# Last sums by column halves, and slots in two parts around a w_in product

## The chip, the core and the metric

The kernel runs on one core of a Trainium2 chip. The core has a matrix engine (TensorE, PE in the profile; PEld is its weight load), VectorE (DVE), ScalarE (ACT), GpSimd (POOL), SyncE (SP, which here only issues DMAs) and 16 DMA engines. SBUF is the on-chip memory with 128 partitions, PSUM holds matmul results in banks. The metric is the device time of one execution in microseconds. Before the change it is 702.29 us, the median of three runs (701.78 to 702.86).

## The reference

For 8 images with 8 heads each, 576 tokens and head size 64, `phi` (576 x 32 per head) is turned into weights by a softmax over the tokens. The weights gather keys and values into 32 memory slots per head; queries attend to the slots; the result, as rows of 512 numbers, goes through an ELU network.

```python
a = exp(phi - max(phi, axis=2)); a = a / (sum(a, axis=2) + 1e-9)
k_m = einsum('bhsm,bhsd->bhmd', a, k)          # 32 slots per head
v_m = einsum('bhsm,bhsd->bhmd', a, v)
attn = softmax(scale * q @ k_m.T)              # over the 32 slots
x = (attn @ v_m) as (4608, 512)
h = x @ w_in                                   # (512, 2048)
g = where(h > 0, h, exp(min(h, 0)) - 1)
out = g @ w_out                                # (2048, 512)
```

## The kernel before

Attention output and `w_in` are never multiplied as such. Per image the kernel forms `vw`, the product of the value slots with `w_in` (L798), in four quarters of 512 columns, and then the hidden rows as probabilities times `vw` (`hidden`, L845). Values that need more than one pass are split into a high and a low part, and products are three passes (HI·HI, LO·HI, HI·LO, the list PASSES).

**Iterations.** From image 2 on each image takes 32 iterations: two halves of 288 tokens, 16 blocks of 128 hidden channels each. `hidden` makes 12 matmuls of 288 columns into one of two banks named psh; ScalarE and VectorE form the ELU (L869, L870, L881, L889); L901 and L907 make the high and low part `gp` of the first 256 tokens; `project` (L923) multiplies both 128-token tiles with `w_out` in 12 matmuls of 512 columns (L915), summed over the 16 blocks in four banks named pso. The last 32 tokens of each half go into a `rest` tile by L889. Over two images there are four such strips of 32, together 128 rows.

**The rest.** After every second image `rest_high` and `rest_low` split two channel blocks at a time, and `rest_project` (L968) adds six matmuls of 512 columns into bank pso00 for each of eight such pairs, 48 in all. `rest_store` (L976) copies the bank into a tile `orest` (L978, ScalarE) and stores it with four DMAs of 32 rows (L982), all four on SP, or, for the last two images, two on SP and two on ACT. Ahead of that the last tiles of the last image are copied (L945, L947) and stored by L950.

**Joint stretches.** Products with 64 rows and 32 columns of weights stand in groups between two projections. In the second such group of images 3 to 6 (`o = base + 2.9`, L1110 on) stand 16 matmuls for quarter 2 of `vw` into the pso banks "y" and "z", 16 for quarter 3 into the two psh banks ("hh"), 144 for the slots of the next image (`next_slots`, L636, into two psb banks, through `slots`, L491 and L505), and 16 for the last scores of this image (`scores_last`, L646), which use the free part of the same psb banks. The copies of the two quarters follow on ScalarE (L810) and VectorE (L816).

**Order.** All orders are written out: the list FIRST up to image 2, and behind it steps with a place, `at(place, step, ...)`, sorted by place and, at one place, by the order of the calls. Each engine runs its instructions in that order; waits between engines come from the tiles that the instructions use.

Of the kernel before, what the change touches and what calls it, by code (L numbers as in the profile page):

```python
# [12 lines left out]
ALU = mybir.AluOpType  # L13
# [3 lines left out]
P = 128  # L17
B, H, S, D, M = 8, 8, 576, 64, 32
DM, DFF = 512, 2048
HALF = S // 2  # L20
NT = HALF // P
REST = HALF - NT * P
# [6 lines left out]
NCH = 5  # L29
NPAIR = H // 2  # L30
NBL = S // 64
NJ = DFF // P
# [142 lines left out]
def fused_kernel(ctx: ExitStack, tc: tile.TileContext, phiT, phi, kv0, kvt, kv, kvb, q0, q1, w_in, w_out, out):  # L175
# [8 lines left out]
    nc = tc.nc  # L184
# [13 lines left out]
    wout = {}  # L198
    def t2k(shape, name):
        return work.tile(shape, F32, name=name, tag="t2k", bufs=7)  # L200
# [47 lines left out]
    def bank(shape, where):  # L248

        pool, name = {  # L250
            "b": (ps_b, "psb"), "h": (ps_h, "psh"),
            "w": (ps_o, "pso00"), "x": (ps_o, "pso01"),
            "y": (ps_o, "pso10"), "z": (ps_o, "pso11"),
        }[where]
        return pool.tile(shape, F32, name=name)
# [17 lines left out]
    def of_blocks(t, u):  # L273
        return t.rearrange("p c (d x) -> p (c d) x", d=2)[:, : min(4, NBL - 4 * u)]
# [48 lines left out]
    def rows_in(b, c, a):  # L323
        r = rows_of(c)
        return slice(a * r, a * r + r) if r < P else slice(0, r)

    def kv_rows(b, c, i, head):
        rows = rows_in(b, c, head % 2)
        if c == 4:
            t = st[b]["kv"]["T" if b == 0 else 4][rows, 0]  # L330
            return t.rearrange("p (i j) d -> p i j d", i=2)[:, i[0] : i[-1] + 1, head // 2, :]
        if b:
            return st[b]["kv"][c][rows, i[0] : i[-1] + 1, head, :]
        return st[0]["kv"]["KV"[i[0]] + str(c // 2)][rows, c % 2 : c % 2 + 1, head, :]
# [156 lines left out]
    def slots(b, c, i=(0, 1), where="bb"):  # L491

        s = st[b]
        if c == 0 and ("slots", i) not in s["ps"]:
            s["ps"]["slots", i] = [bank([P, len(i), D], x) for x in where]
        ps = s["ps"]["slots", i]
        if b >= NB:
            t = s["kv"][c].rearrange("p i h d -> p (i h d)")
            t = t.rearrange("p (c i j d) -> p c i j d", c=2, i=2, j=NPAIR)
            for k in range(2 * c, min(2 * c + 2, NBL)):  # L500
                e = of_blocks(s["e"][k // 4], k // 4)[:, k % 4]
                for a in range(2):
                    for j in range(NPAIR):
                        r = slice(64 * a, 64 * a + 64)
                        nc.tensor.matmul(  # L505
                            ps[a][32 * j : 32 * j + 32],
                            e[r, 32 * j : 32 * j + 32],
                            t[r, k % 2, :, j],
                            start=(k == 0),
                            stop=(k == NBL - 1),  # L510
                            tile_position=(64 * a, 32 * j),
                            skip_group_check=True,
                        )
            return
        for a in range(2):
            rows = rows_in(b, c, a)
            for j in range(NPAIR):
                x = a * P + j * M
                nc.tensor.matmul(
                    ps[a][32 * j : 32 * j + 32],  # L520
                    s["e"][c // 2][rows, c % 2, x : x + M],
                    kv_rows(b, c, i, 2 * j + a),
                    start=(c == 0),
                    stop=(c == NCH - 1),
                    tile_position=(rows.start, 32 * j),
                    skip_group_check=True,
                )
# [108 lines left out]
    def next_slots(b):  # L636

        both = [bank([P, UT + 2 * D], "b") for _ in range(2)]
        st[b]["both"] = both
        st[b + 1]["ps"]["slots", (0, 1)] = [  # L640
            x[:, UT:].rearrange("p (i d) -> p i d", i=2) for x in both
        ]
        for c in range(NCH):
            slots(b + 1, c)

    def scores_last(b):  # L646
        both = st[b].pop("both", None) or [bank([P, UT], "h") for _ in range(2)]
# [186 lines left out]
    gs = {}  # L834
# [75 lines left out]
    acc = {}  # L910
    osbs = {}

    def by_channels(ps, gp, j, first, last):
        for n, (x, y) in enumerate(PASSES):
            nc.tensor.matmul(  # L915
                ps,
                gp[:, y],
                wout[j][:, x, :],
                start=(first and n == 0),
                stop=(last and n == 2),  # L920
            )
# [40 lines left out]
    def rest_low(p, i):  # L962
# [2 lines left out]
            gp[:, LO], gf.rearrange("p j n -> p (j n)"), gp[:, HI], ALU.subtract  # L965
        )

    def rest_project(p, i):  # L968
        if i == 0:
            acc["rest", p] = ps_o.tile([P, DM], F32, name="pso00")  # L970
        gp = gs.pop(("rest", p, i))[1]
        for n in range(2):
            j = 2 * i + n
            by_channels(acc["rest", p], gp[:, :, n * P : (n + 1) * P], j, j == 0, j == NJ - 1)

    def rest_store(p):  # L976
        t = t2k([P, DM], "orest")
        nc.scalar.copy(t, acc.pop(("rest", p)))  # L978

        eng = (nc.sync, nc.scalar) if p == B // 2 - 1 else (nc.sync, nc.sync)  # L980
        for n in range(4):
            eng[n % 2].dma_start(  # L982
                out[2 * p + n // 2, n % 2, NT * P :], t[n * REST : (n + 1) * REST, :]
            )

    tiny = work.tile([P, 1], F32, name="tiny", bufs=1)
    work.tile([P, 24], F32, name="pad_tiny", bufs=1)
# [42 lines left out]
    first = []  # L1030
# [9 lines left out]
    def at(place, f, *a):  # L1040
        if (f, a) not in done:
            plan.append((place, len(plan), f, a))
# [14 lines left out]
    def copies(b, c, *places):  # L1057
        for a, x in enumerate(places):
            at(x, vw_high, b, c, 0, CW, (a,))
            at(x, vw_low, b, c, 0, CW, (a,))  # L1060
# [17 lines left out]
    def slots_done(b, o, *steps):  # L1078
        copied, turned, q_at = (o + x for x in steps)
        at(copied, slots_copy, b)  # L1080
        at(turned, slots_transpose, b)
        at(turned + 0.1, kv_copy, b)
        for u in range(NU):
            at(q_at + u, load_q, b, u)
# [11 lines left out]
    for b in range(3, B):  # L1096
        base = 2 * NJ * b
        o = base - 10.1
        at(o, vw, b, 1, 0, CW, "bb")
        at(o, vw, b, 0, 0, CW, "hh")  # L1100
        at(o, scores_first, b, "wx")
        for c in (1, 0):
            copies(b, c, o, o)
        softmax(b, 0, base - 9.2, 0, 1, 2, 3, 4, 5)
        softmax(b, 1, base - 7.7, 0, 1, 2, 3, 4, 5)
        if b + 1 < B:
            summaries(b + 1, base, -21, -18, -17, -8.2, -16.2, -14, -13)
            slots_done(b + 1, base, 4.3, 7.4, 6)
        softmax(b, 2, base + 1.7, None, 0, 1, 2, 3, 4)
        o = base + 2.9  # L1110
        at(o, vw, b, 2, 0, CW, "yz")
        if b + 1 < B:
            at(o, vw, b, 3, 0, CW, "hh")
            at(o, next_slots, b)
            at(o, scores_last, b)
        else:
            at(o, scores_last, b)
            at(o, vw, b, 3, 0, CW, "bb")
        copies(b, 2, o, o)
        if b + 1 == B:  # L1120
            at(o, turn, b, 3)
        copies(b, 3, o, o)
        softmax(b, 3, base + 5.3, 0 if b + 1 < B else None, 1, 2, 3, 4, 5)
        behind |= {base - 8, base - 7}
        if b + 1 < B:
            behind |= {base + 6, base + 7}
    for it, (b, hf, j) in enumerate(order):
        o = it - 1.35 if it in behind else it - 1.7
        if b > NB:
            o -= 0.96 * (it % 2)  # L1130
        at(o, hidden, it)
        at(o + 0.01, elu_exp, it)
        at(o + 0.02, elu_max, it)
        if b < NB:
            at(it - 1.67, rest_copy, it)
        elif b > NB and b % 2 == 0 and order[max(it - 2, 0)][0] != b:
            at(32 * b - 0.34 + 0.005 * (it - 32 * b), elu_rest, it)
        else:
            at(o + 0.03, elu_rest, it)
        late = 0.695 if it and b != order[it - 1][0] and b % 2 == 0 and b > NB else 0  # L1140
        at(it - 1 + late, elu_high, it)
        at(it - 0.99 + late, elu_low, it)
        at(it + 0.6, project, it)
        if ends[it][2]:
            for t in range(NT):
                at(it + 0.7, collect, it, t)
            if j == NJ - 1:
                at(it + 0.8, store, b, hf)
                if b % 2 and hf:
                    for i in range(NJ // 2):  # L1150
                        at(it + 0.61 + 0.01 * i, rest_high, b // 2, i)
                        at(it + 0.611 + 0.01 * i, rest_low, b // 2, i)
                        at(it + 0.612 + 0.01 * i, rest_project, b // 2, i)
                    at(it + 0.81, rest_store, b // 2)

    plan.sort(key=lambda x: x[:2])
# [50 lines left out]
```

## Time and profile before

| | |
|---|---|
| median of three runs | 702.29 us |
| the profiled execution | 702.28 us |
| its span, first to last instruction | 700.3 us |
| PE, PEld busy | 690.1, 579.7 us |
| DVE, ACT, POOL busy | 460.1, 445.5, 66.2 us |
| HBM read, written | 53.77, 9.44 MB |

The times in the profile are counted from the start of the span. A matmul's busy time includes its way through the array, so several overlap; how fast they follow one another is read from the length of a run of them. A name such as `psb<-kvt,e` gives the tile written and the tiles read.

### The profile page before, as it was taken

To read this page: it belongs to the slowest core of one execution; us is meant where nothing else is said; L and a number is where in the kernel's file an instruction comes from. 1 tells how busy PE (TensorE), PEld (TensorE's weight loads), DVE (VectorE), ACT (ScalarE), POOL (GpSimd) and SP (SyncE) were. 2 spreads that over 40 slices of the span, in tenths; PEclk is the share of its full clock that TensorE was granted. 3 is DMA by queue.
4 is the path that set the end of the run, shared out by engine and by line. 5 is a ranking of instruction groups with operands and counts; after the bars stand their busy time and mean duration, and the time that the engine had idled before them with its cause. 6 is when DMAs were issued, how large, how long until landed. Compare 5 with 4: busy or idle time off the path is not lost.

```text
span 700.3 us, 14400 instructions
## 1 busy us (share of the span) xinstructions
PE 690.1 (99%) x5496; PEld 579.7 (83%) x5496; DVE 460.1 (66%) x1264; ACT 445.5 (64%) x1106; POOL 66.2 (9%) x111
## 2 busy tenths in 40 slices
PE   8999999999999999999999999999999999999997
PEld 7778887888868888888887887888888888878886
DVE  4989887977696558576664666766674655766442
ACT  3879988877457576656655566655664555666552
POOL 0332352123001010001000010000100000000000
PEclk9999999999999999999999999999999999999999
DMA  9992014341404451123202232030501200000001
GB/s 337 407 364 91 1 42 143 101 146 42 137 31 134 168 181 47 49 85 120 85 1 60 90 112 92 31 103 3 174 29 46 69 1 31 1 31 1 30 1 46
DMA packets 24220, 64.14 MB, mean 92 GB/s; under 512 B 3288, under 2 KB 4824, under 8 KB 24152
## 3 DMA queue, kind: packets, MB, share of 16 engines
q1 hardware_dynamic: 23480, 63.06, 25.8%
q8 instruction: 44, 0.72, 0.4%
q10 hardware_dynamic: 672, 0.16, 0.1%
q14 instruction: 24, 0.20, 0.1%
HBM read 53.77 MB, written 9.44 MB: 90 GB/s over the span
## 4 chain that ended last, share of the span: by engine, by line
PE 94%; DMA 4%; DVE 0%; issue 0%; ACT 0%; SPq 0%
PE pso L915 57%; PE psh L854 29%; PE psb L578 3%; PE psb L505 2%; DMA raw<-w_out 2%; PE pso L578 2%; DMA raw<-w_in 1%; PE psh L578 1%; DMA qh<-q 1%; DMA touch<-kv 0%; PE psb L591 0%; PE pso L591 0%; PE psb L547 0%; PE psh L734 0%; SPq L321 0%
## 5 line engine op out<-in xcount | busy, mean ns | idle before, releaser
L915 PE MATMUL pso<-wout,gp 128*128 128x512 f32 x1728 | 426.8, 393 | 0.0
L915 PEld LDWEIGHTS pso<-wout,gp 128*128 128x128 f32 x1728 | 314.2, 188 | 66.5 <-issue 4.0
L854 PEld LDWEIGHTS psh<-A,vw 128*128 128x128 f32 x1536 | 218.4, 188 | 19.4 <-DVE gp L907 2.5
L854 PE MATMUL psh<-A,vw 128*128 128x288 f32 x1536 | 230.4, 295 | 0.7 <-ACT A L777 0.4
L869 ACT ACTIVATE gf<-psh 128x288 f32<-128x288 f32 x256 | 104.6, 409 | 120.8 <-PE psh L854 118.0
L881 DVE SCALAR_TENSOR_TENSOR gf<-gf,psh 128x256 f32<-128x256 f32 x192 | 80.3, 418 | 115.9 <-ACT gf L870 115.8
L907 DVE TENSOR_TENSOR gp<-gf,gp 128x256 fp32r<-128x256 f32 x256 | 113.2, 445 | 29.0 <-ACT gp L901 27.0
L901 ACT CAST gp<-gf 128x256 fp32r<-128x256 f32 x256 | 101.5, 401 | 34.1 <-DVE gf L881 17.3
L870 ACT ACTIVATE gf<-gf 128x288 f32<-128x288 f32 x256 | 113.9, 445 | 8.1
L293 POOL TENSOR_TENSOR e<-e,nmb 128x512 f32<-128x512 f32 (+1 forms) x18 | 19.1, 1081 | 291.9 <-DMA e<-phi 97.6
L878 DVE SCALAR_TENSOR_TENSOR gf<-gf,psh 128x288 f32<-128x288 f32 x64 | 28.5, 450 | 17.1 <-ACT gf L870 15.4
L889 DVE SCALAR_TENSOR_TENSOR rest<-gf,psh 128x32 f32<-128x32 f32 x192 | 34.6, 180 | 0.0
L816 DVE TENSOR_TENSOR vw<-psb,vw 128x512 fp32r<-128x512 f32 (+2 forms) x40 | 20.9, 561 | 14.3 <-ACT vw L810 14.3
L959 ACT CAST gp<-rest 128x256 fp32r<-128x256 f32 x32 | 13.0, 406 | 25.1 <-PE pso L915 25.1
L964 DVE TENSOR_TENSOR gp<-rest,gp 128x256 fp32r<-128x256 f32 x32 | 13.3, 421 | 18.8 <-ACT gp L959 18.5
L897 POOL COPY rest<-gf 128x32 f32<-128x32 f32 x64 | 18.7, 319 | 71.2 <-DVE gf L878 71.2
L810 ACT CAST vw<-psb 128x512 fp32r<-128x512 f32 (+2 forms) x40 | 17.5, 488 | 11.8 <-PE psb L578 11.6
L395 ACT ACTIVATE mag<-raw 128x512 uint32<-128x512 uint32 x30 | 20.0, 669 | 2.7 <-DVE win L417 1.4
L391 ACT ACTIVATE mag<-raw 128x512 f32<-128x512 f32 x30 | 19.7, 667 | 1.3 <-DMA raw<-w_in 1.0
L578 PE MATMUL psb<-win,kvm 64*32 64x512 f32 (+2 forms) x320 | 17.9, 505 | 0.0
L816 DVE TENSOR_TENSOR vw<-pso,vw 128x512 fp32r<-128x512 f32 (+1 forms) x18 | 10.1, 597 | 9.9 <-ACT vw L810 9.8
L505 PEld LDWEIGHTS psb<-kvt,e 64*32 64x32 f32 x864 | 12.6, 105 | 3.3 <-issue 3.3
(144 smaller groups left out, 474.1 us busy)
## 6 DMA issues: line engine op xcount, KB each, us to landing
kvt<-kvb SPq DMA_DIRECT2D x24, 512.0 KB, 4.8
raw<-w_in SPq DMA_DIRECT2D x15, 512.0 KB, 8.0
raw<-w_out SPq DMA_DIRECT2D x15, 512.0 KB, 10.0
out<-osb SPq DMA_DIRECT2D x14, 512.0 KB, 2.8
qt<-q SPq DMA_DIRECT2D x18, 384.0 KB, 4.3
kvt<-kv SPq DMA_DIRECT2D x8, 512.0 KB, 8.9
ph<-phiT SPq DMA_DIRECT2D x7, 576.0 KB, 5.6
e<-phi SPq DMA_DIRECT2D x12, 256.0 KB, 3.4
```

The lines of the kernel that those rows point to most:

```text
L505: nc.tensor.matmul(ps[a][32 * j : 32 * j + 32], e[r, 32 * j : 32 * j + 32], t[r, k % 2, :, j], start=(k == 0), stop=(k == NBL - 1), tile_p ...
L578: nc.tensor.matmul(outs[a][32 * j : 32 * j + 32, :], lhs[r, 32 * j : 32 * j + 32], rhs[r, j], start=True, stop=True, tile_position=(64 * a ...
L816: nc.vector.tensor_tensor(t[:, LO, a, n0:n1], s["ps"]["vw", c, n0][a], t[:, HI, a, n0:n1], ALU.subtract)
L854: nc.tensor.matmul(ps, t[:, x, g, c0 : c0 + P], s["A"][hf][:, y, g, :], start=(n == 0), stop=(n == 5),)
L869: nc.scalar.activation(gf, ps, AF.Relu, scale=-1.0)
L870: nc.scalar.activation(gf, gf, AF.Exp, scale=-1.0)
L878: nc.vector.scalar_tensor_tensor(gf, gf, -1.0, ps, ALU.add, ALU.max)
L881: nc.vector.scalar_tensor_tensor(gf[:, :n], gf[:, :n], -1.0, ps[:, :n], ALU.add, ALU.max)
L889: nc.vector.scalar_tensor_tensor(rest_of(b, j)[:, o : o + REST], gf[:, n:], -1.0, ps[:, n:], ALU.add, ALU.max)
L901: nc.scalar.copy(gp[:, HI], gs[it][:, : NT * P])
L907: eng.tensor_tensor(gp[:, LO], gf[:, : NT * P], gp[:, HI], ALU.subtract)
L915: nc.tensor.matmul(ps, gp[:, y], wout[j][:, x, :], start=(first and n == 0), stop=(last and n == 2),)
```

## The change

Two edits that don't touch each other.

In the second joint stretches `next_slots` makes only the matmuls of the first of five chunks (32), the second chunk (32) follows, then quarter 3 of `vw`, then the other three chunks (80), then the scores.

At the end of the kernel the last two channel blocks of the last pair of images are no longer summed into pso00. That bank is complete after block 13; ScalarE copies it to `orest`. Blocks 14 and 15 go into half banks of 256 columns, columns 256 to 511 first, then 0 to 255; VectorE adds each half into `orest`; the first half is stored by one DMA of 128 rows on SP, the second by two DMAs of 64 rows, one on SP, one on ACT. This step stands behind the last tiles' copies and store. The rest of the other three pairs of images is stored by one DMA of 128 rows in place of four.

```diff
@@ next_slots
-        for c in range(NCH):
-            slots(b + 1, c)
+        slots(b + 1, 0)
@@ by_channels
-    def by_channels(ps, gp, j, first, last):
+    def by_channels(ps, gp, j, first, last, n0=0, n1=DM):
...
-                wout[j][:, x, :],
+                wout[j][:, x, n0:n1],
@@ rest_project, rest_store
+    HALF_DM = DM // 2
+
     def rest_project(p, i):
         if i == 0:
             acc["rest", p] = ps_o.tile([P, DM], F32, name="pso00")
-        gp = gs.pop(("rest", p, i))[1]
-        for n in range(2):
-            j = 2 * i + n
-            by_channels(acc["rest", p], gp[:, :, n * P : (n + 1) * P], j, j == 0, j == NJ - 1)
+        gp = gs["rest", p, i][1]
+        ps = acc["rest", p]
+        of = [(2 * i + n, gp[:, :, n * P : (n + 1) * P]) for n in range(2)]
+        if p < B // 2 - 1 or i < NJ // 2 - 1:
+            last = NJ - 1 if p < B // 2 - 1 else NJ - 3
+            for j, g in of:
+                by_channels(ps, g, j, j == 0, j == last)
+            return
+
+        t = t2k([P, DM], "orest")
+        nc.scalar.copy(t, ps)
+        for n in (1, 0):
+            half = bank([P, HALF_DM], "h")
+            cols = slice(n * HALF_DM, (n + 1) * HALF_DM)
+            for j, g in of:
+                by_channels(half, g, j, j == 2 * i, j == NJ - 1, cols.start, cols.stop)
+            nc.vector.tensor_tensor(t[:, cols], half, t[:, cols], ALU.add)
+            if n:
+                nc.sync.dma_start(rest_rows(p)[:, :, cols], t[:, cols])
+            else:
+                rows = slice(0, P // 2), slice(P // 2, P)
+                for eng, r, h in ((nc.sync, rows[0], slice(0, 2)), (nc.scalar, rows[1], slice(2, 4))):
+                    eng.dma_start(rest_rows(p)[h, :, cols], t[r, cols])
+
+    def rest_rows(p):
+        return out[2 * p : 2 * p + 2, :, NT * P :].rearrange("b h r n -> (b h) r n")
 
     def rest_store(p):
-        t = t2k([P, DM], "orest")
-        nc.scalar.copy(t, acc.pop(("rest", p)))
-
-        eng = (nc.sync, nc.scalar) if p == B // 2 - 1 else (nc.sync, nc.sync)
-        for n in range(4):
-            eng[n % 2].dma_start(
-                out[2 * p + n // 2, n % 2, NT * P :], t[n * REST : (n + 1) * REST, :]
-            )
+        if p < B // 2 - 1:
+            t = t2k([P, DM], "orest")
+            nc.scalar.copy(t, acc["rest", p])
+            nc.sync.dma_start(rest_rows(p), t)
@@ second joint stretches
         at(o, vw, b, 2, 0, CW, "yz")
         if b + 1 < B:
+            at(o, next_slots, b)
+            at(o, slots, b + 1, 1)
             at(o, vw, b, 3, 0, CW, "hh")
-            at(o, next_slots, b)
+            for c in range(2, NCH):
+                at(o, slots, b + 1, c)
             at(o, scores_last, b)
@@ places of the rest
-                        at(it + 0.612 + 0.01 * i, rest_project, b // 2, i)
+                        last = 0.2 if b + 1 == B and i == NJ // 2 - 1 else 0
+                        at(it + 0.612 + 0.01 * i + last, rest_project, b // 2, i)
```

## Rows read from the trace of the kernel before

**Rows 1.** The page: busy times, one DMA queue, one group of instructions.

```profile
PE 690.1 (99%) x5496; PEld 579.7 (83%) x5496; DVE 460.1 (66%) x1264; ACT 445.5 (64%) x1106; POOL 66.2 (9%) x111
...
q8 instruction: 44, 0.72, 0.4%
...
L881 DVE SCALAR_TENSOR_TENSOR gf<-gf,psh 128x256 f32<-128x256 f32 x192 | 80.3, 418 | 115.9 <-ACT gf L870 115.8
```

**Rows 2.** Stage windows, images 4 and 6: length, busy time of each engine.

```profile
380.57:385.43 4.86, 4.58 (x194) 2.91 (x193) 3.26 (x8) 2.65 (x6) 0.00 (x0) 1.00 0.28 75
...
545.61:549.86 4.25, 4.25 (x194) 2.84 (x193) 2.69 (x7) 2.66 (x6) 0.00 (x0) 1.00 0.19 27
```

**Rows 3.** Chain in order of time, images 4 and 5: start, length, what.

```profile
384.25 0.28 issue
...
457.98 1.02 PE pso L578 x16
459.00 0.86 PE psh L578 x16
459.86 2.03 PE psb L505 x134
461.89 0.34 PE psb L578 x15
```

**Rows 4.** Chain in order of time, the last 25 us.

```profile
678.17 1.56 PE psh L854 x12
679.73 16.52 PE pso L915 x72
```

**Rows 5.** Timeline of the last 10 us: start, length, engine, line.

```profile
696.27 0.58 ACT L978 COPY orest<-pso 128x512 f32<-128x512 f32 x1 [3.25 <-PE pso L915]
696.88 0.80 SPq L982 DMA_DIRECT2D out<-orest  x2
696.88 0.85 ACTq L982 DMA_DIRECT2D out<-orest  x2
```

**Rows 6.** Timeline around image 5's second joint stretch.

```profile
459.04 1.07 ACT L810 CAST vw<-pso 128x512 fp32r<-128x512 f32 x2 [1.24 <-PE pso L578]
...
459.66 1.29 DVE L816 TENSOR_TENSOR vw<-pso,vw 128x512 fp32r<-128x512 f32 x2 [1.56 <-ACT vw L810]
...
460.87 1.28 DVE L816 TENSOR_TENSOR vw<-psh,vw 128x512 fp32r<-128x512 f32 x2
...
462.06 0.42 DVE L907 TENSOR_TENSOR gp<-gf,gp 128x256 fp32r<-128x256 f32 x1
...
464.80 1.73 PEld L854 LDWEIGHTS psh<-A,vw 128*128 128x128 f32 x12
```

**Rows 7.** Timeline around image 4's second joint stretch.

```profile
380.57 0.18 DVE L889 SCALAR_TENSOR_TENSOR rest<-gf,psh 128x32 f32<-128x32 f32 x1
...
384.53 0.26 PEld L505 LDWEIGHTS psb<-kvt,e 64*32 64x32 f32 x20 [0.54 <-issue]
```

**Rows 8.** DMA view, 40 slices each of 381.3 to 383.2 and 456.2 to 457.4.

```profile
DMA  0600000000009000000000000000000000000000
...
DMA  0000900000000000000000000000000000000000
```

**Rows 9.** DMA view: whole span; from 322.6, 694.4 and 697.6 on (with slices).

```profile
DMA packets 24220, 64.14 MB, mean 92 GB/s; under 512 B 3288, under 2 KB 4824, under 8 KB 24152
...
DMA packets 12, 0.00 MB, mean 2 GB/s; under 512 B 12, under 2 KB 12, under 8 KB 12
...
DMA packets 272, 0.52 MB, mean 308 GB/s; under 512 B 16, under 2 KB 16, under 8 KB 272
...
GB/s 0 0 0 351 117 176 293 117 468 59 117 59 352 234 293 117 176 351 176 117 59 117 411 351 351 527 117 645 117 235 351 351 117 59 59 59 0 0 0 0
DMA packets 192, 0.26 MB, mean 187 GB/s; under 512 B 64, under 2 KB 64, under 8 KB 192
```

**Rows 10.** Stage window inside the last tiles' store; last columns DMA share, GB/s.

```profile
694.55:695.95 1.40, 1.40 (x8) 1.03 (x6) 0.00 (x0) 0.00 (x0) 0.00 (x0) 1.00 0.98 369
```

## The prediction

> **What bounds the kernel now.** I read the page's busy shares first [rows 1]: TensorE (PE) is busy 99% of the 700.3 us span, and the chain of waits that ended last is nearly all PE. So an edit counts only if it changes what PE streams, makes PE wait, or changes what comes behind PE's last matmul. Both halves of the change touch such places, so next come the stage windows of the four second joint stretches (images 3 to 6, between one product with w_out and the next) and the chain through one of them, then the last 10 us as timeline and as DMA windows.
>
> In the stretches three of the four windows are 4.25 us long and PE is busy through all of it; the one of image 4 is 4.86 with 4.58 busy [rows 2]. The chain through image 5's shows the pieces in a row, with no idle time: w_in quarter 2 takes 1.02 (its first matmuls follow a change of tile form), quarter 3 0.86, the slots 2.03, the scores 0.34 [rows 3]. At the end of the kernel the chain is PE to 696.25, then 0.58 of ScalarE copy, then two DMA issues on each of SP and ACT, then only DMA [rows 4, 5].
>
> **The stretches: order alone.** The change moves 64 of the slots' 144 matmuls in front of the w_in quarter 3. Nothing is added. 16 matmuls of 512 columns take 0.86 and 144 of 128 columns 2.03 [rows 3]: 1.7 and 1.6 ns per column of each, the same rate, so PE is bound by the columns it streams whichever comes first, and both have the same 64x32 tile form, so no change of form is added. The sum on PE is zero.
>
> What moves behind PE: quarter 3 ends later by 64/144 of 2.03, 0.90 us. Its two ScalarE copies and two VectorE subtractions now start that much later, and queued behind them are ELU's casts (L901) on ScalarE and L907 on VectorE. VectorE works back to back from 459.66 on [rows 6], with quarter 2's parts until 460.95; quarter 3's first part would then wait for its copy, so VectorE loses about 0.6 and not 0.9: L907 then ends at about 463.1 instead of 462.48. Who waits: the second projection behind the stretch, whose third matmul (the low part) comes near 463.9 (six matmuls of 0.23 from 462.2, a little longer for the first, then two more). About 0.8 us is left. The two psh banks come free near 462.7 instead of 462.15, and the next product into them loads weights at 464.80 [rows 6]: 2 us left. If these covers were gone the price would be up to 0.9 per stretch, 3.6 in all; I take zero. The slots' key-value buffers come free up to 0.9 earlier, so SP issues the next q loads earlier; they feed the next image, tens of us on. That is no gain.
>
> One stretch has a real hole: image 4's slots stand still for 0.54 us (0.28 on the chain) with no engine named [rows 3, 7]. PE's instructions arrive as 16 KB packets on queue 8 (44 of them [rows 1] for 2 x 5496 records, some 250 instructions each). In this stretch a packet comes at 381.87 and the hole ends 2.66 later; in image 5 the packet comes at 456.3, ahead of the stretch, and there is no hole [rows 8]. I read the hole as PE outrunning its instructions. In the old order quarter 3's weight loads wait for psh, which VectorE's L889 frees at 380.75 [rows 7], and PE's program stands there; in the new order slots, which wait for nothing so late, stand in that place, so the request may go out earlier. Bounds: the hole goes (-0.6, the difference of the windows) or a second stretch gets one (+0.6). I take -0.2, a third of what there is.
>
> **The tail: PE, copy and add.** Now six matmuls of 512 columns end the kernel's PE work, 16.52/72 = 0.229 each [rows 4]. They become twelve of 256, each between half of that, 0.115, and 0.130 (a 288-column matmul: 1.56/12, [rows 4]); I take 0.12, so 1.44 instead of 1.38. The old accumulator is complete at 694.87; ScalarE's copy of it (0.58) lies beside the first half. The halves end at 695.6 and 696.3. Each is followed by a VectorE add of 128x256 out of PSUM, 0.42 by the nearest row [rows 1] (0.32 to 0.64 by half and all of a 512-column one, 1.28/2 [rows 6]). The first store is issued at 696.07, the last two, one on SP and one on ACT, at 696.8. Now the first pair goes out at 696.88 and the second 0.4 later [rows 5]. Up to here the change gains: 0.1 on the first issue, 0.5 on the last.
>
> **The tail: the transfers.** Here I expect the loss. The full store of 512 KB shows 272 packets: 256 of 2 KB and 16 under 512 B, as many as there are DMA engines. I read the small ones as one closing packet of each engine that took part. The last four 32-row stores show 64 small ones, 16 each. But the small DMA at L282, whose target in memory has an outermost dimension of 4 (eight runs of 128 B, 1.0 KB), shows 12 packets: 8 and only 4 [rows 9]. So a DMA can land on four engines, and this one differs from the others in the outer dimension of its target. The new stores write (b h) r n with the four (b, h) outermost, then the two of a half: the first would run on 4 engines, the last two on 2 each. The old ones had 32 rows outermost and ran on 16.
>
> The Trainium skill ("DMA: Bandwidth & Descriptors", section on why a DMA increments its semaphore by 16) states that as a rule: the engine count is the largest number up to 16 that divides the slowest dimension of both sides. The rows agree (4 for L282, 16 for the rest). It also says that they are always the lowest-numbered ones, which no row here shows.
>
> Price: with all 16 engines full the store moves 369 GB/s [rows 10], 23 GB/s per engine, so 1 KB costs 44 ns at that rate; small packets won't be better, and I take 47. Each of the first half's four engines gets 32 packets, each of the last two DMAs' two engines 32. If all three start from the same engine, the two busiest carry 96: 4.5 us. If they fall on different engines, 32: 1.5 us. No row shows the choice; I take 96, because a choice that follows from shape alone (six of six L282s took four) needs no memory of what ran before. The first packet comes 0.83 after its issue (696.88 to the fourth slice of the last window, [rows 5, 9]), so at 696.9; the last at 701.4 instead of 698.9 (slice 36 of the window from 697.6 to 699.0). What follows the last packet is the same 1.4 us to the end of the span. So the tail costs +2.5.
>
> The other pairs' rest stores also become one DMA on four engines, 256 KB at 4 x 23 GB/s = 2.8 us each. Nothing waits for them: the buffer is one of seven. SP saves three issues each. Zero, and if they delayed an instruction packet, up to 0.5 once.
>
> **Sum.** 702.28 (the profiled execution, 2 us above its span, and 0.01 below the median) + 2.5 - 0.2 = 704.6 us.
>
> **Rivals.** (1) The stores spread over all engines after all. Then eight packets per engine, 0.4 us, behind first packets at 697.6 to 697.9: the last ends near 698.2, 0.7 earlier than now, and with the stretch 701.4. This is the case that does not get slower; it decides where the number of small packets in the tail is 16 per DMA. For it: of the page's 3288 packets under 512 B [rows 9], 512 are those of the four touch loads (128 each) and 48 those of the six L282; the 2728 left are 16 for each of 169 DMAs and 4 for each of six, so 169 of 175 DMAs ran on all engines. Against it: the only targets of this form are the six, and none of them did. (2) Narrow, but on different engines: the ACT store's packets run 697.9 to 699.4, +0.5, so 702.6. (3) The second add waits until the first half's store has read the tile, since both use one tile. The add then starts at 698.4 at the earliest, its stores' first packet comes at 699.7, and 64 packets per shared engine end at 702.7: 705.9. Against it: ScalarE still copies the second part into a vw tile until 460.11 while VectorE works on the first from 459.66 [rows 6], so parts of a tile are told apart there; a DMA as the reader is not shown. (4) The covers in the stretches break or two holes appear: 705 to 708.
>
> **Chances.** Main case 0.60, (1) 0.20, (2) 0.08, (3) 0.07, (4) 0.05. The main case's own range is 703.9 to 705.4 (44 to 54 ns per packet, the hole gone or kept). The whole range reaches down into rival (1): 701.2 to 705.6. A measurement of this kernel can tell about 0.2%, 1.4 us, from no change: slower begins at 703.7. Slower: main case, (3) and most of (4), less noise: 0.65. Faster needs more than rival (1) gives at its centre: 0.07. Within: 0.28.
>
> **What would show it.** Right: in the tail's DMA window three DMAs of 1 KB packets with 4 + 2 + 2 small packets, a DMA share well under 0.3 for over 4 us, the last landing near 701.4, with PE's last matmul at 696.2 to 696.5. Wrong: 16 small packets per DMA and a last packet before 698.5 (rival 1); a last add near 698.4 (rival 3). For the stretches: four windows of 4.25, or 4.86 still at image 4; any wait of PE for gp or psh behind them refutes the covers.

## The result, and the profile after

The changed kernel takes 706.28 us (median of six runs, 705.87 to 706.46) where the kernel before takes 701.80 in the same comparison: ratio 1.0059, 95% interval 1.0046 to 1.0072. The forecast was 704.6, within 701.2 to 705.6. So it is slower, as said, but it lies 0.7 us above the range.

The profiled execution takes 705.96 (before 702.28), its span is 703.7 (700.3). These two lie 3.68 apart and the medians 4.48; 29 more executions of the kernel before, beside e1 to e4, have a median of 702.39, which is 3.9 under 706.28. First the page: TensorE's busy time and the engine shares are within 1% of what they were, and 236 small packets are gone, as many as sixteen rest stores with 16 closing packets each (256) less three with 4 and one each with 4, 2 and 2 (20).

```profile
PE 689.3 (98%) x5502; PEld 581.8 (83%) x5502; DVE 460.9 (65%) x1266; ACT 445.9 (63%) x1106; POOL 66.0 (9%) x111
...
DMA packets 24112, 64.14 MB, mean 91 GB/s; under 512 B 3052, under 2 KB 4844, under 8 KB 24044
...
q8 instruction: 44, 0.72, 0.4%
```

Next the chain that ended last (start, length, what), which answers to [rows 4], and the timeline behind it, which answers to [rows 5].

```profile
679.24 15.12 PE pso L914 x66
694.36 1.45 PE psh L914 x12
695.81 0.02 issue
695.84 0.42 DVE orest L988
```

```profile
694.40 0.59 ACT L982 COPY orest<-pso 128x512 f32<-128x512 f32 x1 [1.87 <-PE pso L914]
695.19 0.42 DVE L988 TENSOR_TENSOR orest<-psh,orest 128x256 f32<-128x256 f32 x1 [2.08 <-PE psh L914]
695.64 0.58 SPq L990 DMA_DIRECT2D out<-orest  x1
695.84 0.42 DVE L988 TENSOR_TENSOR orest<-psh,orest 128x256 f32<-128x256 f32 x1 [0.23 <-PE psh L914]
696.31 0.53 SPq L994 DMA_DIRECT2D out<-orest  x1
696.34 1.34 ACTq L994 DMA_DIRECT2D out<-orest  x1
```

PE, copy, adds and issues are as forecast: 12 matmuls of 0.121, two adds of 0.42, the last two issues at 696.3, 0.5 behind PE's last matmul. Then the DMA view of the tail, 40 slices from 696.8 to 702.4:

```profile
DMA  1231132223222112011201101011111111100000
GB/s 37 37 29 29 66 95 80 73 95 95 80 95 59 44 44 37 22 37 51 44 22 44 29 22 44 29 44 51 51 44 44 59 44 44 59 22 22 22 29 0
DMA packets 264, 0.26 MB, mean 47 GB/s; under 512 B 8, under 2 KB 264, under 8 KB 264
...
q1 hardware_dynamic: 198, 0.20, 12.9%
q10 hardware_dynamic: 66, 0.07, 3.3%
```

The 256 KB that before were 192 packets in 1.2 us [rows 9] run for 5.5 us at 47 GB/s, with a DMA share of 0.1 to 0.3. There are 8 small packets for three DMAs: 6 on SP's queue (198 less 192 of data), 2 on ACT's. Read one by one, the closing packets come at 698.60, 698.60, 698.79 and 698.90 (first half), 700.38 and 700.93 (SP's second), 701.74 and 702.29 (ACT's): 4 + 2 + 2 engines. SP's second store has its first packets right behind the closings at 698.79 and 698.90, and ACT's right behind those at 700.38 and 700.93, so all three queue on the same two engines.

Last the stage windows of the four second joint stretches, images 3 to 6 (length, then busy time of PE, PEld, DVE, ACT, POOL, clock, DMA share, GB/s), which answer to [rows 2]:

```profile
292.79:297.09 4.30, 4.30 (x193) 3.15 (x192) 2.29 (x6) 2.51 (x6) 0.00 (x0) 1.00 0.35 119
380.55:384.95 4.40, 4.40 (x193) 3.11 (x192) 2.40 (x6) 2.61 (x6) 0.00 (x0) 1.00 0.43 121
457.38:461.68 4.30, 4.30 (x193) 3.15 (x192) 2.29 (x6) 2.51 (x6) 0.00 (x0) 1.00 0.37 109
545.15:549.43 4.27, 4.27 (x193) 3.08 (x192) 2.27 (x6) 2.49 (x6) 0.00 (x0) 1.00 0.39 104
```

Image 4's hole is all but gone in this execution (4.40 for 4.86), the other three are 0.02 to 0.05 longer; no wait of PE for gp or psh follows. PE's last matmul ends 0.43 earlier than before (695.80 for 696.23). The span grows by 3.44: 3.87 behind that matmul, less 0.43.

### The profile page after: what moved, and what is told of

Its sections match the earlier page's. It is cut to its first block, busy times and chain, and to the rows that moved or that the text cites. A ratio compares the mean times of both kernels' runs of the same rounds, so it can differ in the third digit from the quotient of the medians.

```text
span 703.7 us, 14404 instructions
## 1 busy us (share of the span) xinstructions
PE 689.3 (98%) x5502; PEld 581.8 (83%) x5502; DVE 460.9 (65%) x1266; ACT 445.9 (63%) x1106; POOL 66.0 (9%) x111
## 4 chain that ended last, share of the span: by engine, by line
PE 95%; DMA 1%; DVE 1%; ACT 1%; issue 0%; SPq 0%; DVEq 0%
PE pso L914 56%; PE psh L853 29%; PE psb L578 3%; PE psb L505 2%; PE pso L578 2%; PE psh L578 1%; DMA kvt<-kv 1%; PE pso L591 1%; PE pso L1031 1%; DMA touch<-kv 0%; PE psb L547 0%; PE psb L591 0%; PE psh L519 0%; PE pso L519 0%; PE psh L914 0%
```

## Experiments

Two questions: does the tail's loss come from the number of engines, and does the order of the stretches gain anything? The last two columns are us behind PE's last matmul, read from each kernel's trace; the ratios are to the kernel before, on the same chip. Edits are shown in part, with what repeats itself left out.

| kernel | ratio (95%) | closing packets per DMA | last packet | end |
|---|---|---|---|---|
| before | 1 | 16 | 2.72 | 4.04 |
| changed | 1.0059 (1.0046 to 1.0072) | 4, 2, 2 | 6.50 | 7.91 |
| e2 tail alone | 1.0057 (1.0044 to 1.0070) | 4, 2, 2 | 6.37 | 7.79 |
| e3 halves in blocks | 0.9993 (0.9985 to 1.0002) | 16 | 2.54 | 3.88 |
| e4 first half narrow | 1.0010 (1.0002 to 1.0019) | 4, then 16 | 3.23 | 4.86 |
| e5 old tail, one store | 1.0048 (1.0030 to 1.0066) | 4 | 6.26 | 7.68 |
| e6 last two on SP | 1.0043 (1.0029 to 1.0056) | 4, 2, 2 | 6.48 | 7.83 |
| e7 no first store | 1.0040 (1.0026 to 1.0054) | 2, 2 | 5.36 | 6.76 |
| e8 rows outermost | 0.9989 (0.9980 to 0.9998) | 16 | 2.42 | 3.85 |

**e1 and e2: one half of the change each.** e1 is the old kernel with the new order of the stretches, e2 the changed kernel with the old order:

```
 e1 (before +)                           e2 (changed kernel, back to)
+at(o, next_slots, b)                    +at(o, vw, b, 3, 0, CW, "hh")
+at(o, slots, b + 1, 1)                   at(o, next_slots, b)
 at(o, vw, b, 3, 0, CW, "hh")            -at(o, slots, b + 1, 1)
...                                      ...
```

> Before, with the new order in the second joint stretches alone (the tail as it was). Theory (the order gains by the hole of image 4 alone: windows of 4.40 instead of 4.85, and 4.30, 4.30, 4.27 instead of three times 4.25): 0.3 us less than before, 701.5, PE's last matmul near 695.8, the tail behind it unchanged at 4.0. Rival (the order costs something later that the tail covers in the changed kernel, or its gain was chance): 0 or more, 701.8 to 702.5.

> The changed kernel with the old order in the second joint stretches: the tail's edit alone. Theory (the whole loss is the tail, 3.8 us behind PE's last matmul in the profiled execution): 706.6, ratio to before near 1.006, a hole of 0.5 again in image 4. Rival (part of the loss is in the stretches): 704.6 to 705.5.

e2: 706.28, the whole loss is the tail. e1: 702.01 for 702.39, ratio 0.9995 (0.9986 to 1.0003), no difference that can be told; and its hole is not gone, image 4's window is 4.94 (below). So the new order by itself does not remove the hole.

**e3 and e4: the halves stay, the engines come back.**

```
 e3: for both halves                     e4: for the second half only
+for g in range(4):
+    eng = (nc.sync, nc.scalar)[g % 2]
+    r = slice(g * REST, (g + 1) * REST)
+    eng.dma_start(out[2 * p + g // 2, g % 2, NT * P :, cols], t[r, cols])
```

> The changed kernel, but both column halves are stored in blocks of 32 rows, four DMAs each, in turn on SP and ACT: targets with 32 outermost, so 16 engines each. Theory (the loss is the number of engines): 16 closing packets per DMA, last packet 2.3 to 2.7 us behind PE's last matmul (before: 2.65), so with the order's 0.3 between 700.8 and 701.6. Rival A (the halves with their adds and the longer row of PE, add, DMA cost the time, however the transfer spreads): 703 or more. Rival B (1 KB packets are slow to start on any number of engines): last packet 3.5 us or more behind PE, 702.5.

> The changed kernel, but only the second column half is stored in blocks of 32 rows (16 engines); the first half goes out as one DMA of 128 rows (4 engines). Theory (engines share: the four carry 32 packets of the first half and then 8 of the second): first half's packets from 1.2 us after its issue to about 2.1 us later, then 8 packets of 45 ns; the last packet 3.2 us behind PE's last matmul, so 701.9 to 702.6. Rival (the ACT queue waits for SP's ring as a whole, whatever the engines): last packet 4 us or more behind PE, 703 or more.

e3 has the same halves, adds and 1 KB packets, five DMAs more, and the loss is gone: 701.86, last packet at 2.54. Both its rivals fall (703, and 3.5 us). e4 pays for one narrow DMA out of three: last packet at 3.23 as expected, 0.5 more than before's, the time 702.97, a little over the expected 702.6.

**e5: one narrow store alone.** The kernel before, its last four stores made one.

```
-for n in range(4): ... out[2 * p + n // 2, n % 2, NT * P :], t[n * REST : (n + 1) * REST, :]
+nc.sync.dma_start(out[2 * p : 2 * p + 2, :, NT * P :].rearrange("b h r n -> (b h) r n"), t)
```

> Before, with one edit: the last pair's rest goes out as one DMA of 128 rows of 2 KB (target with 4 outermost) instead of four of 32 rows; no halves, no adds, the old stretches. Theory (the number of engines is the loss): 4 closing packets; issue 0.65 behind PE's last matmul, first packet 1.2 later, 32 packets of 2 KB on each of four engines in 4.2 us (as the changed kernel's middle stores ran), last packet near 6.1, end 7.4 behind PE instead of 4.0: 3.4 us more than before. Rival (the halves, their adds and three stores are the loss): within 0.5 us of before.

705.80, 3.5 us more than before; the rival (within 0.5) falls. The DMA view of e5, 698.4 to 702.9:

```profile
GB/s 18 91 18 73 18 0 0 0 36 18 0 0 18 0 36 55 73 55 73 55 73 73 91 109 91 127 73 127 91 73 146 73 127 91 91 91 55 55 36 0
DMA packets 132, 0.26 MB, mean 58 GB/s; under 512 B 4, under 2 KB 4, under 8 KB 132
```

128 packets of data and 4 small ones. From the middle on each engine moves one packet of 2 KB in 84 ns, 24 GB/s, close to the 23 that the prediction took from a full store [rows 10]; but the first 1.5 us hold only a few packets. One by one, most of each engine's first four to eight take 0.09 to 0.93 us instead of 0.084. The changed kernel's middle stores (p below 3) start in the same way.

**e6 and e7: who waits for whom on the two engines.**

```
 e6: -(nc.scalar, rows[1], slice(2, 4))      e7: -nc.sync.dma_start(rest_rows(p)[:, :, cols], t[:, cols])
     +(nc.sync, rows[1], slice(2, 4))            +continue
```

> The changed kernel with the ACT store of the second half issued on SP too: three DMAs on one queue, the same engines. Both theories: 96 packets in a row on two engines. Theory R (a queue's next DMA is not fetched ahead, so each DMA on it pays its own start and stalls, 55 to 66 ns per packet, and the ACT one at 42 ns had been fetched): the last 32 packets take 2.0 us instead of 1.4, end 8.4 to 8.6 behind PE's last matmul (changed kernel 7.9). Theory C (the stalls in SP's second store came from ACT's being fetched on the same engines): 42 to 46 ns per packet in both, end 7.2 to 7.4.

> The changed kernel without the store of the first column half: columns 256 to 511 of the last pair's rest rows are left unwritten. Theory (two engines, one DMA behind the other on each): SP's 32 packets per engine from 1.7 us behind PE's last matmul to 3.6, ACT's then to 5.0 to 5.6, end 6.4 to 7.0 behind PE: 1.0 to 1.5 less than the changed kernel. Rival (the last two lie on different engines, or run beside each other): ACT's packets begin by 2.2 and end by 4.0, end 5.3 or less.

e7 came out as the theory said: SP's packets go from 1.7 to 3.99 behind PE, ACT's start at 3.97, when SP's are through, although they were issued in the same 0.03 us. Its DMA view from 700.75 on, with SP's last three packets in it:

```profile
GB/s 53 27 53 53 53 53 26 53 53 53 53 53 26 53 53 53 53 53 26 53 53 53 53 53 26 53 53 53 53 26 53 53 53 53 53 27 0 0 0 0
...
q10 hardware_dynamic: 66, 0.07, 11.9%
q1 hardware_dynamic: 3, 0.00, 0.3%
```

ACT's 64 packets run evenly, two engines at 42 ns per KB. e6 fitted neither theory. With all three DMAs on SP the end is 7.83, not 8.4 and not 7.3: the third one's packets come at 42 ns though it is on the same queue (against R), the second one's 32 take 1.5 us on one of its engines and 2.2 on the other (against C on that one, as no other queue is there). What the packets show in the changed kernel, e5, e6 and e7 is this: in the narrow DMA that finds the engine idle some packets take up to 0.93 us, most of them the first four and then every fourth; the second of three has some of these on one of its two engines (32 packets in 2.1 us, 1.5 on the other), and the last of two or three has none. Why the early packets are slow stays open.

**e8: the same three stores, other order of dimensions.** The rest's 128 columns are laid so that partition 4r+g holds row r of (b, h) g.

```
+def places(b, hf, j):
+    g = b % 2 * 2 + hf
+    return rest_of(b, j).rearrange("p (r g) -> p r g", g=4)[:, :, g]
-rest_of(b, j)[:, o : o + REST]          +places(b, hf, j)
-.rearrange("b h r n -> (b h) r n")      +.rearrange("b h r n -> r (b h) n")
```

> The changed kernel with the rest's columns laid row by row over the four (b, h) instead of one (b, h) after another, so that partition 4r+g holds row r of (b, h) g and the same three stores of 128 and 64 partitions have targets with 32 or 16 outermost, then 4. Nothing else differs in the tail: same halves, adds, queues, packets of 1 KB. Theory (the outermost dimension of the target sets the engines): 16 closing packets per DMA; last packet 2.2 behind PE's last matmul, end 3.5 to 3.6 (changed kernel 7.9, before 4.0): 701.2 to 702.0 where before has 702.3. Rival (one DMA over four separate places is narrow or slow in any order): end 6 or more behind PE, 704 or more. VectorE's and GpSimd's writes of the rest now step 16 B and may take longer; they have slack, so nothing is expected of that.

701.62 for 702.30; the end is 3.85 behind PE's last matmul, a little over the expected 3.6. This is the cleanest proof: queues, partitions, packet size, halves and adds are those of the changed kernel, and what differs is the order of the rows, in the tile and so in the target. Timeline of e8's issues, then its DMA view from 697.7 to 699.2:

```profile
696.51 0.59 SPq L992 DMA_DIRECT2D out<-orest  x1
696.71 0.42 DVE L990 TENSOR_TENSOR orest<-psh,orest 128x256 f32<-128x256 f32 x1 [0.22 <-PE psh L916]
697.19 0.57 SPq L996 DMA_DIRECT2D out<-orest  x1
697.21 0.66 ACTq L996 DMA_DIRECT2D out<-orest  x1
```

```profile
GB/s 0 137 137 273 382 355 355 328 328 300 437 219 137 82 28 0 0 0 0 191 164 164 191 300 246 191 328 164 219 219 382 192 219 109 191 28 0 0 0 0
DMA packets 304, 0.26 MB, mean 175 GB/s; under 512 B 48, under 2 KB 304, under 8 KB 304
```

48 small packets for three DMAs, 16 each. The first half is over before the second begins; they take 0.5 and 0.6 us. Its first packet comes 1.2 us after the issue (696.51 to slice 1, 697.74), as in the changed kernel, so that delay does not come from the number of engines; SP's 64-partition store in e7 has it too (1.21), the 32-partition ones before have 0.83. And its first half, which finds the engines idle, has no slow packets: they take 44 to 61 ns each, 8 to an engine (46 in the even stretches of the narrow stores, where they start 42 apart). So the narrow DMAs cost more than their 96 steady packets (4.1 us): they have slow packets too, which this one has not. e8 is 0.1% faster than the kernel before, at the edge of what the interval can tell, and 0.7% faster than the changed one by the two ratios.

**e9 to e11: the hole.** A place, below, is the number of a TensorE record (matmul, weight load or sequencer's) counted from the start of its stretch. e9 is e8 with 36 more warm-up matmuls at the start (one execution, 706.95), e10 is e8 with the old order and 6 more, e11 is e1 once more.

```
 e9: -warm_up.3 ... warm_up.2 ... warm_up.6 warm_up.3 ... warm_up.2 ... warm_up.8
     +warm_up.9 ... warm_up.8 ... warm_up.12 warm_up.9 ... warm_up.8 ... warm_up.14
 e10: -warm_up.8     +warm_up.14     and the stretches as in e2
```

> e8 with 36 more warm-up matmuls of 128 columns in the first 40 us, where TensorE waits for loads: every later TensorE instruction stands 72 places further back in its 256-instruction packets. Theory (the hole is a packet boundary reached 256 instructions after the one before, faster than the packet comes): the stretches in which two boundaries lie under 2.5 us apart are now image 3's and image 6's, at places 110 and 366 and at 67 and 323, instead of image 4's at 51 and 307; one or both of their windows show 0.1 to 0.7 us more than 4.27 at those places, and image 4's is 4.27 or 4.30. Rival (the hole belongs to image 4's data or to its q loads): it stays there.

> e8's tail with the old order in the stretches and 6 more warm-up matmuls: boundaries 12 places earlier in the stretches, so that no two lie under 2.58 us apart (2.46 in image 4 before). Theory: windows of 4.25 four times, or one up to 0.3 longer; tail 3.85 behind PE's last matmul; 0.2 to 0.9 us under before, ratio 0.9987 to 0.9997. Rival (the new order was worth something itself): 702 or more, slower than e8 by 0.3 or more.

> e1 a second time, for the trace alone. If the hole's length belongs to the program, image 4's window is 4.94 again; if it belongs to when the packet happens to come in that execution, it lies anywhere from 4.27 to 4.95 and follows the packet: no hole where it comes within 0.95 us of the stretch's start.

Stage windows, one line of each kernel: image 4 in e1, e11 and e3, image 4 and 5 in e9, image 4 and 6 in e10.

```profile
380.21:385.15 4.94, 4.57 (x193) 3.11 (x192) 2.93 (x7) 2.76 (x6) 0.00 (x0) 1.00 0.43 121
```

```profile
380.34:384.87 4.53, 4.53 (x193) 3.10 (x192) 2.52 (x6) 2.75 (x6) 0.00 (x0) 1.00 0.42 126
```

```profile
380.29:384.56 4.27, 4.27 (x193) 3.07 (x192) 2.27 (x6) 2.48 (x6) 0.00 (x0) 1.00 0.39 108
```

```profile
385.10:389.38 4.27, 4.27 (x193) 3.07 (x192) 2.29 (x6) 2.48 (x6) 0.00 (x0) 1.00 0.36 109
...
461.83:466.87 5.04, 4.75 (x193) 3.17 (x192) 3.06 (x8) 2.76 (x6) 0.00 (x0) 1.00 0.48 154
```

```profile
382.03:386.27 4.25, 4.25 (x193) 2.84 (x192) 2.71 (x7) 2.65 (x6) 0.00 (x0) 1.00 0.17 27
...
546.41:551.46 5.05, 4.68 (x193) 2.90 (x192) 3.46 (x9) 2.66 (x6) 0.00 (x0) 1.00 0.32 90
```

e1 and e11 are one program, 4.94 and 4.53: the hole's length belongs to the execution. And it moves with the count of PE's instructions. Before, it stands at the 6592nd of PE's records, 256 x 26 - 64; with blocks of 256 counted from there, image 4's stretch has boundaries at its places 51 and 307, 2.5 us apart. A warm-up matmul of float32 shows as two matmuls and two weight loads (e9's page has 72 more of each than e8's), so e9 shifts by 144 places and e10 by 24, not by 72 and 12, and the images that I named were the wrong ones. With the true shifts, worked out after the runs, image 5 has a pair of boundaries at 126 and 382 in e9 and image 6 one at 115 and 371 in e10, and within two records of 382 and 371 the holes are (0.62 and 0.69), and image 4 has none. The rival (it belongs to image 4) falls. A close pair alone makes no hole: in e9 image 3 has one too, 38 and 294, 2.4 us apart, and no hole; its packet begins 0.28 before the stretch. The timeline of weight loads shows e9's and e10's:

```profile
466.46 0.10 PEld L578 LDWEIGHTS psb<-qt,kvm 64*32 64x32 f32 x1 [0.67 <-issue]
```

```profile
551.00 0.15 PEld L578 LDWEIGHTS psb<-qt,kvm 64*32 64x32 f32 x7 [0.74 <-issue]
```

What differs between executions is when the packet comes (its start). 40 slices, 2 us in all, from the start of image 4's stretch, e1 and then e3; the 16 KB packet is the 9 on the right:

```profile
DMA  0000000000000000000030000000000000090000
```

```profile
DMA  0000000000000006009000000000000000000000
```

It comes 1.77 us after the start in e1 and 0.92 in e3, which has no hole. Of the eleven executions with these places (e1 to e8, e11, before, changed) the three with the packet at 0.90 to 0.94 lose 0 to 0.13 in that window, e11, at 0.97, loses 0.26, and the seven from 1.06 on lose 0.3 to 0.7. Nor does a hole need a close pair: behind image 6's stretch in e7 the boundaries are at places 139 and 395, 4 us apart, the packet comes at 3.13 (2.3 to 2.7 in the other executions of this order), and PE stands for 0.51 at 395:

```profile
551.61 1.46 PEld L914 LDWEIGHTS pso<-wout,gp 128*128 128x128 f32 x7 [0.94 <-issue]
```

In every hole of these stretches PE goes on 2.3 to 3.1 us after the packet's start. That fits a hole wherever the packet is late for PE's next boundary; that PE waits for just this packet the profile doesn't name.

Neither e9 nor e10 is a gain in time. In e9 the added matmuls hold up the start (image 3's stretch begins at 297.36, in e8 at 293.41). e10 missed its range, with 1.0000 (0.9990 to 1.0009) for 0.9987 to 0.9997 and a window 0.8 longer instead of 0.3 at most. In its profiled execution image 3's stretch begins at 294.33, but that can't be put down to the 6 matmuls: the granted clock of its first 60 us is 0.97 (1.00 in e8), 3.4 us of them at half.

```profile
0.00:60.00 60.00, 54.18 (x668) 46.30 (x669) 42.62 (x106) 39.47 (x95) 14.56 (x25) 0.97 0.83 323
```

By its numbers (702.58, e8 701.62) e10's rival came in, that the new order is worth something; but the two intervals overlap, and window 6 alone lost 0.8, so no run shows it.

## Why the prediction came out wrong

**Right.** PE, copy and adds (1.44 forecast, 1.45; no wait of the second add for the first store, so rival 3 falls). The mechanism of the loss: 4, 2 and 2 engines, all from the same first ones, 96 packets on each of two (rivals 1 and 2 fall; e8 and e5 show that the target's outermost dimension does it). The 1.4 us from last packet to end (1.40; before 1.33). The covers in the stretches held (rival 4), and the other pairs' narrow stores cost nothing that shows.

The Trainium skill's rule ("DMA: Bandwidth & Descriptors", section on why a DMA increments its semaphore by 16) speaks of the slowest dimension of both sides; e8 agrees, 128 and 64 partitions with targets of 32 and 16 outermost closing with 16 packets. That the engines are the lowest-numbered no run shows by number; that DMAs of two engines queue behind one another on the same pair, e7 shows.

**Wrong: the size of the transfer term.** The step said 47 ns per packet of 1 KB, from a rate with all engines full [rows 10], and a first packet 0.83 after its issue, from a 32-row DMA [rows 5, 9]. Last packet forecast: 5.1 behind PE's last matmul (701.4 less 696.3); measured 6.50. Of the 1.4, 0.38 is the first packet (1.21 after the issue instead of 0.83), 0.95 the packets (5.45 us for 96, 57 ns each) and 0.07 the issue. The steady packet is indeed 42 ns; 96 of them are 4.1 us. The other 1.4 us are the slow packets of the first and second DMA. The 32-row stores before have some too (87 to 173 ns for 84 in the first two of each engine), e8's 16 engines have none. The rate of a full store, with data behind it at every moment, left them out, and the first packet came from a DMA of another shape. With them the tail is +3.9, and the range, whose main case ended at 54 ns per packet, missed the result.

**Wrong in its reason: the stretch.** The -0.2 was meant for the hole; 0.45 went in the profiled execution, but the reason given, a wait for psh, isn't there. psh is free at 380.75 [rows 7], and the weight loads that should wait for it start at 381.03, 0.46 after the stretch's start; the slots' that take their place in the changed kernel start 0.46 after it too:

```profile
381.03 0.15 PEld L578 LDWEIGHTS psh<-win,kvm 64*32 64x32 f32 x8 [0.28 <-issue]
```

```profile
381.01 0.15 PEld L505 LDWEIGHTS psb<-kvt,e 64*32 64x32 f32 x8 [0.28 <-issue]
```

Whether the order moves the request in another way stays open. PE's weight loads pass place 51 at 0.9 in both orders, its matmuls at 1.00 in the new and 1.32 in the old one. The packet comes at 1.26 to 1.35 in the three executions with the old order, which lose 0.34 to 0.61 (mean 0.52), and at 0.90 to 1.77 in the eight with the new one, which lose 0 to 0.67 (mean 0.32). That leans the way of the forecast, but eleven executions don't settle it, and e1 and e11 show that one program can have either. Against it, windows without a hole are 0.02 to 0.17 longer in the new order (4.27 to 4.42 for 4.25). How much went in the profiled execution was in part luck, and e1's interval tells no difference in time.

Sum by these terms: 702.28 + 3.87 - 0.43, and 0.24 more outside the span (705.96 less 703.7, for 702.28 less 700.3), is 705.96, the profiled execution.

## What to carry to other kernels

A store that several small ones are merged into can be slower than all of them: look at what stands outermost in its target, and count the closing packets in the trace. Where the order of rows in the tile is free, lay them so that a long dimension comes first (e8); then one DMA serves as well as four. For a DMA at the end of a kernel take the delay to the first packet and the pace of the early ones from a DMA of the same shape on as many engines, not the rate of a full stream.

## Not expected of the hardware

- DMAs of 64 and 128 partitions had their first packet 1.21 to 1.26 us after the issue (e7, changed, e8, e5), those of 32 partitions 0.83 [rows 5, 9]; SP's issues took 0.53 to 0.63 and 0.34 to 0.42.
- Packets of narrow DMAs on idle engines took up to 0.25 us (1 KB, changed) and 0.93 (2 KB, e5) at first, for 0.046 and 0.084 later; e8's first DMA on 16 idle engines had 0.044 to 0.061 from the start.
- Two narrow DMAs from two queues, issued within 0.03 us, run one after the other on their common engines (e7: 3.99 and 3.97), not packet by packet.
- ACT's issue of a two-engine DMA took 1.34 us beside SP's 0.53 (1.38 beside 0.57 in e7); e8's 16-engine one took 0.66. It cost nothing here, as its packets had to wait anyway.
- PE can outrun its own program: it stood for up to 0.7 us at counts of 256 instructions, most often where two of them lay about 2.5 us apart, once where they lay 4 us apart (e7), and went on 2.3 to 3.1 us after the start of a 16 KB packet. The Trainium skill ("Runtime: NRT & Kernel Launch", section "Instruction fetch mechanics") calls the cost of a block boundary mostly hidden. These traces agree for nearly all of the 44, and show where it isn't: short instructions with two boundaries in one stretch, or a late packet (e7).
